# A retention layer and a gated FFN on one core: W3 times W_out moved to the head, 256-token FFN tiles, k padded in place of q

## The chip, the cores and the metric

The kernel runs on one core of a Trainium2 chip. Five engines work side by side, each with an instruction queue of its own that it takes in order: TensorE (PE, matmuls into the eight PSUM banks), VectorE (DVE), ScalarE (ACT), GpSimd (POOL) and SyncE (SP, which issues all loads and stores here). The metric is the device time in microseconds, as the median of several executions.

## The reference

A linear attention over 4 batches, 8 heads, 768 positions and head size 64, with a decay per head, gives `x`; a gated feed-forward follows.

```python
gamma = 1.0 - 2.0 ** (-5.0 - np.arange(H))
for t in range(S):
    state = gamma * state + einsum('bhd,bhe->bhde', k[:, :, t], v[:, :, t])
    y[:, :, t] = einsum('bhd,bhde->bhe', q[:, :, t], state) / sqrt(D)
x = y.transpose(0, 2, 1, 3).reshape(3072, 512)
a, b = x @ w1, x @ w2            # 512 x 1024 each
out = ((a * b) @ w3) @ w_out     # 1024 x 1024, 1024 x 512
```

## The kernel before

The recurrence is cut into 24 steps of 128 positions (6 for each batch). For each, a chunk of q, k and v (256 KB each, in float32) is loaded by `load_chunk(n)`, up to six ahead. `casts(n)` makes float16 copies: q on ScalarE, k on GpSimd, and v times the decay (`vp`, zero-padded per pair of heads) on GpSimd. `transposes(n)` turns q and k with TensorE into one PSUM bank (`psT`); VectorE copies k and q out (`kT`, `qT`), and ScalarE copies q a second time, in two halves of 64 partitions, into a zero-padded `qp`. `scores(n)` multiplies `kT` and `qp` into `psA`, and VectorE masks them (`am`). `kv(n)` makes the new state (`psK`, then `s` on VectorE and `t` on GpSimd); the last step of a batch has none. `outputs(n)` adds both parts in `psY`, the first step of a batch without a state, and VectorE writes them, scaled, into `XT`, which keeps x transposed for all 3072 tokens in float16.

Since nothing stands between w3 and w_out, the kernel multiplies these two first: `w3_transpose(f)` and `w3_mm(f)` make row f of `W3O` (1024 x 512), and the FFN then needs only `out = (a * b) @ W3O`. In units: `a_unit` multiplies a tile of tokens by 128 columns of w1 into one bank (`psF`), which ScalarE copies out (`pa`); `b_unit` does it for w2, and VectorE multiplies `pa` by it straight from the bank (`ht`); `o_unit` multiplies 128 tokens of `ht` by `W3O`, ScalarE scales the result (`osb`), and SyncE stores it. `psF` has three banks, `pa` two buffers.

The order is written out by hand. In the head, chunks 0 and 1 are loaded first, then half of w1 and w2, chunks 2 and 3, the other half, chunks 4 and 5, w_out and w3, through six staging buffers; steps 0 to 5 run among the first three FFN tiles, and then W3O is made in one piece (16 matmul groups in a row). From step 6 on `step(n)` runs a queue of FFN units: it pulls a quarter of its share after the transposes, after the scores, after psK and after psY. Tiles are 256 tokens for the first five and the last, 512 for the three between. `step` places the transposes of n + 1 ahead of the scores of n:

```python
casts(n + 1 + look)
transposes(n + 1)
fill.pull(share * 0.25, ready)
scores(n)
fill.pull(share * 0.25, ready)
t_new = kv(n)
fill.pull(share * 0.25, ready)
outputs(n, t_new)
fill.pull(share * 0.25, ready)
```

Of the kernel before, what the change touches and what calls it, by code (L numbers as in the profile page):

```python
# [18 lines left out]
def kernel(  # L19
# [11 lines left out]
    nc = tc.nc  # L31
    B, H, S, D = q.shape
    C = 128
    NCH = S // C
# [11 lines left out]
    wstage = ctx.enter_context(tc.tile_pool(name="wstage", bufs=6))  # L46
# [34 lines left out]
    def load_w12(half):  # L81

        got = []
        for d in range(4):
            t = new_stage()
            for i, w in enumerate((moe_w1, moe_w2)):
                dma_in(
                    t[:, i * 512 : (i + 1) * 512],
                    w[d * 128 : (d + 1) * 128, half * 512 : (half + 1) * 512],
                )  # L90
            got.append(t)
        return got
# [25 lines left out]

    ident16 = const.tile([128, 128], HP, name="ident16")
# [45 lines left out]
    W12 = [wpool.tile([128, 2, 2, 512], HP, name=f"w12_{i}") for i in range(4)]  # L167
# [11 lines left out]
    def cast_w12(half, got):  # L179
        for d in range(4):  # L180
            cast_to(W12[d][:, half, :, :].rearrange("p a n -> p (a n)"), got[d][:, :], d % 2 == 0)

    def cast_wo(got, i):
        cast_to(WO[i][:, :, :].rearrange("p a n -> p (a n)"), got[i][:, :], False)

    def cast_w3(got, f):
        t = att.tile([128, 1024], HP, tag="w3h", name="w3h", bufs=4)
        cast_to(t[:, :], got[f][:, :], f % 2 == 0)
        W3h[f] = t


    def w3_transpose(f):
        src = W3h.pop(f)
        ps = ps_t.tile([128, 1024], HP, tag="psT", name="psT")
# [4 lines left out]
        t = att.tile([128, 1024], HP, tag="w3t", name="w3t")  # L199
        nc.vector.tensor_copy(t[:, :], ps[:, :])  # L200
        w3t[f] = t

    def w3_mm(f):
# [7 lines left out]
        nc.scalar.copy(W3O[f][:, :], ps[:, :])  # L211


    q16s, k16s, qTs, kTs, ATs = {}, {}, {}, {}, {}
    Tst = [None]

    def casts(n):
# [4 lines left out]
        nc.scalar.copy(q16[:, :], q32[:, :])  # L222
# [13 lines left out]
    def transposes(n):  # L236
# [4 lines left out]
        for p in range(NP):  # L241
            nc.tensor.transpose(ps[:, 0, p, :], q16[:, p * 128 : (p + 1) * 128], ident16[:, :])  # L242
        for p in range(NP):
            nc.tensor.transpose(ps[:, 1, p, :], k16[:, p * 128 : (p + 1) * 128], ident16[:, :])  # L244
        qp = QP[n % 2]
        qT = att.tile([128, NP, 128], HP, tag="qT", name="qT")
        kT = att.tile([128, NP, 128], HP, tag="kT", name="kT")
# [4 lines left out]
        qTs[n], kTs[n] = qT, kT  # L252

    def scores(n):
        kT, qp = kTs.pop(n), QP[n % 2]
        am = att.tile([128, NP, 2, 128], HP, tag="am", name="am")
        for half in range(2):
            ps = ps_at.tile([128, 2, 2, 128], FP, tag=f"psA{half}", name=f"psA{half}")
            for i in range(2):
                p = half * 2 + i  # L260
                nc.tensor.matmul(  # L261
                    ps[:, i, :, :], lhsT=kT[:, p, :], rhs=qp[:, p, :, :], start=True, stop=True
                )
# [44 lines left out]

    class Ffn:
        def __init__(self, tok0, TB, bufs):  # L310
            self.tok0, self.TB, self.bufs = tok0, TB, bufs
            self.HT = None

        def mm(self, which, f):
            half, col = f // 4, (f % 4) * 128
            ps = ps_f.tile([128, self.TB], FP, tag="psF", name="psF")
            for d in range(4):
                nc.tensor.matmul(  # L318
                    ps[:, :], lhsT=W12[d][:, half, which, col : col + 128],
                    rhs=XT[:, d, self.tok0 : self.tok0 + self.TB],  # L320
# [4 lines left out]
        def a_unit(self, f):  # L325
            if self.HT is None:
                TB = self.TB
                self.HT = fsb.tile([128, 8, TB], HP, tag=f"ht{TB}", name=f"ht{TB}", bufs=self.bufs)
            ps = self.mm(0, f)
            self.pa = fsb.tile([128, self.TB], FP, tag="pa", name="pa")  # L330
            nc.scalar.copy(self.pa[:, :], ps[:, :])  # L331

        def b_unit(self, f):
            ps = self.mm(1, f)
            nc.vector.tensor_tensor(self.HT[:, f, :], self.pa[:, :], ps[:, :], MULT)  # L335
# [205 lines left out]
```

## Time and profile before

| what | value |
|---|---|
| time, median of 3 runs | 222.26 us (222.25 to 222.26) |
| the profiled execution's own time | 223.81 us |
| its span, first to last instruction | 222.1 us |
| mean granted TensorE clock | 0.975 of full speed |
| busy: TensorE, VectorE, ScalarE, GpSimd | 194.0, 125.0, 104.0, 65.1 us |
| TensorE in the chain that ended last | 77% of the span |

Busy time adds up what an engine's instructions took; a TensorE at half clock is busy too, and pipelined matmuls overlap in it. The chain follows the work that ended last backwards, at each step to what released it. The granted clock is that of the throttle: 1.00 is 2.4 GHz, 0.50 is 1.2 GHz, a value between is a mean over a stretch that has both.

### The profile page before, as it was taken

How to read it: one execution, taken by the hardware profiler on the slowest of the kernel's cores; microseconds unless marked ns; L12 is line 12 of the kernel's file. 1: busy time of each engine (PE TensorE's matmuls, PEld its weight loads, DVE VectorE, ACT ScalarE, POOL GpSimd, SP SyncE). 2: the span in 40 equal slices, each digit the busy share in tenths (PEclk: the TensorE clock that was granted, in tenths of full speed). 3: DMA queues.
4: the chain of work that ended last, by engine and by line, in shares of the span. 5: the costliest groups of instructions: out<-in, count | busy, mean ns of one | idle time of the engine just before them, and what ended most of it. 6: DMA issues, size and time to landing. Idle time of an engine off the chain costs nothing.

```text
span 222.1 us, 4183 instructions
## 1 busy us (share of the span) xinstructions
PE 194.0 (87%) x1536; PEld 128.3 (58%) x1536; DVE 125.0 (56%) x244; ACT 104.0 (47%) x194; POOL 65.1 (29%) x114
## 2 busy tenths in 40 slices
PE   0366769688999989988999999999999999999992
PEld 0254647577755545677777665665556555457650
DVE  4595655574653334466968877678666654431210
ACT  5333515557733484355465554554654443333231
POOL 5514525120004403324673554542045202000000
PEclk9997976999999999999999999999999999999999
DMA  7999999905999963999459996790630011111212
GB/s 144 241 336 214 283 265 274 400 24 192 282 238 218 222 132 116 260 197 219 65 128 227 204 228 147 182 215 3 146 90 35 17 47 50 47 47 47 97 77 111
DMA packets 82899, 35.91 MB, mean 162 GB/s; under 512 B 75712, under 2 KB 75712, under 8 KB 82880
## 3 DMA queue, kind: packets, MB, share of 16 engines
q1 hardware_dynamic: 82880, 35.66, 68.0%
q8 instruction: 12, 0.20, 0.4%
q14 instruction: 7, 0.06, 0.1%
HBM read 29.36 MB, written 6.29 MB: 161 GB/s over the span
## 4 chain that ended last, share of the span: by engine, by line
PE 77%; ACT 7%; SPq 4%; issue 4%; DVE 4%; DMA 3%; ACTq 0%; DVEq 0%
PE psF L318 35%; PE psO L340 19%; PE psW L207 5%; SPq L60 4%; PE psA L261 4%; DMA q<-in_q_dram 3%; PE psT L242 3%; PE psT L244 2%; ACT qp L251 2%; PE psY L299 2%; PE psY L300 2%; PE psY L302 2%; PE psK L282 2%; PE psT L196 1%; ACT pa L331 1%
## 5 line engine op out<-in xcount | busy, mean ns | idle before, releaser
L318 PE MATMUL psF<-xt,w 128*128 128x256 f16 (+1 forms) x576 | 99.1, 316 | 6.5 <-ACT pa L331 3.0
L318 PEld LDWEIGHTS <-w 128*128 128x128 f16 x576 | 56.1, 101 | 30.7 <-issue 5.7
L335 DVE TENSOR_TENSOR ht<-pa,psF 128x256 f16<-128x256 f32 (+1 forms) x72 | 36.5, 508 | 44.7 <-ACT pa L331 19.9
L331 ACT COPY pa<-psF 128x256 f32<-128x256 f32 (+1 forms) x72 | 31.3, 444 | 33.5 <-PE psF L318 32.4
L340 PE MATMUL psO<-w3o,ht 128*128 128x512 f16 x192 | 45.0, 379 | 0.0
L291 POOL TENSOR_TENSOR t<-s,GS 128x512 f16<-128x512 f32 x16 | 20.3, 1269 | 63.6 <-DVE s L290 48.3
L264 DVE TENSOR_TENSOR am<-psA,keep 128x512 f16<-128x512 f32 x48 | 30.9, 685 | 8.9 <-PE psA L261 8.8
L345 ACT ACTIVATE osb<-psO 128x512 f32<-128x512 f32 x24 | 14.3, 597 | 40.7 <-PE psO L340 39.3
L228 POOL TENSOR_TENSOR vp<-v,VS 128x256 f16<-128x256 f32 x48 | 28.5, 615 | 10.4 <-PE psY L302 4.4
L340 PEld LDWEIGHTS <-ht 128*128 128x128 f16 x192 | 18.3, 98 | 18.6
L224 POOL CAST k<-k 128x512 f16<-128x512 f32 x24 | 14.9, 620 | 45.2 <-DMA k<-in_k_dram 30.7
L250 ACT COPY qp<-psT 64x512 f16<-64x512 f16 x24 | 13.9, 578 | 25.5 <-DVE qT L249 10.7
L261 PE MATMUL psA<-qp,kT 128*128 128x256 f16 x96 | 14.8, 278 | 7.9 <-ACT qp L251 7.1
L248 DVE COPY kT<-psT 128x512 f16<-128x512 f16 x24 | 10.1, 421 | 16.5 <-PE psT L244 16.5
L299 PE MATMUL psY<-am,vp 128*128 128x128 f16 x96 | 17.4, 224 | 1.4 <-DVE am L264 1.0
L303 DVE TENSOR_TENSOR xt<-psY,YS 128x512 f16<-128x512 f32 x24 | 16.5, 687 | 3.0 <-PE psY L302 3.0
L300 PE MATMUL psY<-am,vp 128*128 128x128 f16 x96 | 17.4, 225 | 0.0
L261 PEld LDWEIGHTS <-kT 128*128 128x128 f16 x96 | 9.5, 100 | 12.8 <-issue 7.1
L242 PE MATMUL psT<-ident,q 128*128 128x128 f16 x96 | 10.0, 230 | 7.3 <-ACT q L222 7.3
L207 PE MATMUL psW<-wo,w3t 128*128 128x512 f16 x64 | 15.1, 379 | 0.0
L222 ACT CAST q<-q 128x512 f16<-128x512 f32 x24 | 14.8, 618 | 0.0
L302 PE MATMUL psY<-qT,t 128*128 128x128 f16 x80 | 14.8, 221 | 0.0
(43 smaller groups left out, 157.1 us busy)
## 6 DMA issues: line engine op xcount, KB each, us to landing
q<-in_q_dram SPq DMA_DIRECT2D x24, 256.0 KB, 4.9
k<-in_k_dram SPq DMA_DIRECT2D x24, 256.0 KB, 5.0
v<-in_v_dram SPq DMA_DIRECT2D x24, 256.0 KB, 4.8
out_dram<-osb SPq DMA_DIRECT2D x24, 256.0 KB, 2.0
stg<-in_moe_w_dram SPq DMA_DIRECT2D x16, 256.0 KB, 5.6
stg<-in_moe_w_dram SPq DMA_DIRECT2D x8, 512.0 KB, 5.0
stg<-in_moe_w_out_dram SPq DMA_DIRECT2D x4, 512.0 KB, 6.1
```

Of the source, the lines that this page charges most:

```text
L207: nc.tensor.matmul(ps[:, :], lhsT=t[:, g * 128 : (g + 1) * 128], rhs=WO[g // 2][:, g % 2, :], start=(g == 0), stop=(g == 7),)
L228: nc.gpsimd.tensor_tensor(vp[:, :, r, r * 64 : r * 64 + 64], v32[:, :].rearrange("j (p s e) -> j p s e", s=2, e=64)[:, :, r, :], VS[:, :]. ...
L261: nc.tensor.matmul(ps[:, i, :, :], lhsT=kT[:, p, :], rhs=qp[:, p, :, :], start=True, stop=True)
L264: nc.vector.tensor_tensor(am[:, half * 2 : half * 2 + 2, :, :].rearrange("j p s i -> j (p s) i"), ps[:, :, :, :].rearrange("j p s i -> j ( ...
L291: nc.gpsimd.tensor_tensor(t16[:, :, :], s32[:, :, :], GS[:, :, :], MULT)
L299: nc.tensor.matmul(ps[:, p, :], lhsT=vp[:, p, 0, :], rhs=am[:, p, 0, :], start=True, stop=False)
L300: nc.tensor.matmul(ps[:, p, :], lhsT=vp[:, p, 1, :], rhs=am[:, p, 1, :], start=False, stop=(c == 0))
L302: nc.tensor.matmul(ps[:, p, :], lhsT=Tst[0][:, p, :], rhs=qT[:, p, :], start=False, stop=True)
L318: nc.tensor.matmul(ps[:, :], lhsT=W12[d][:, half, which, col : col + 128], rhs=XT[:, d, self.tok0 : self.tok0 + self.TB], start=(d == 0), ...
L331: nc.scalar.copy(self.pa[:, :], ps[:, :])
L335: nc.vector.tensor_tensor(self.HT[:, f, :], self.pa[:, :], ps[:, :], MULT)
L340: nc.tensor.matmul(psO[:, :], lhsT=self.HT[:, f, tb * 128 : (tb + 1) * 128], rhs=W3O[f][:, :], start=(f == 0), stop=(f == 7),)
```

## The change

The order of the head is new. w3 row 0, w_out, and w3 rows 1 to 4 are loaded first, then chunks 0 and 1, w3 rows 5 to 7, w1 and w2 in whole rows (1024 columns), and chunks 2 to 5; the staging pool has 12 buffers. W3O is made first, with steps 0 and 1 inside it, and its transposes use a `psF` bank. Matmuls on zeros (`busy`, 8 and 10) stand around the first W3 transposes. The first FFN tile runs by rows: all eight column blocks of w1 row d at once, in three `psF` banks and the `psY` bank, then w2 in the same way; ScalarE copies the w1 sums into two staging buffers. From step 2 on all is in the queue, and all tiles have 256 tokens. k is padded (`kp`) by ScalarE's two copies, no longer q, VectorE copies only qT, k is transposed ahead of q, and the scores are 8 matmuls of 128 columns. q is cast on GpSimd.

```diff
-    wstage = ctx.enter_context(tc.tile_pool(name="wstage", bufs=6))
+    wstage = ctx.enter_context(tc.tile_pool(name="wstage", bufs=WST))
...
+    w3_st = [load_rows(moe_w3, 0)]
+    wo_st = [load_wo(i) for i in range(4)]
+    w3_st += [load_rows(moe_w3, f) for f in range(1, 5)]
     load_chunk(0)
     load_chunk(1)
+    w3_st += [load_rows(moe_w3, f) for f in range(5, 8)]
+    w1_st = [load_rows(moe_w1, d) for d in range(4)]
+    w2_st = [load_rows(moe_w2, d) for d in range(4)]
+    for n in range(2, 6):
+        load_chunk(n)
...
-        nc.scalar.copy(q16[:, :], q32[:, :])
+        nc.gpsimd.tensor_copy(q16[:, :], q32[:, :])
...
-        nc.vector.tensor_copy(kT[:, :, :], ps[:, 1, :, :])
+        nc.scalar.copy(kp[0:64, :, 0, :], ps[0:64, 1, :, :])
+        nc.scalar.copy(kp[64:128, :, 1, :], ps[64:128, 1, :, :])
         nc.vector.tensor_copy(qT[:, :, :], ps[:, 0, :, :])
-        nc.scalar.copy(qp[0:64, :, 0, :], ps[0:64, 0, :, :])
-        nc.scalar.copy(qp[64:128, :, 1, :], ps[64:128, 0, :, :])
...
-                nc.tensor.matmul(
-                    ps[:, i, :, :], lhsT=kT[:, p, :], rhs=qp[:, p, :, :], start=True, stop=True
-                )
+                for r in range(2):
+                    nc.tensor.matmul(
+                        ps[:, i, r, :], lhsT=kp[:, p, r, :], rhs=qT[:, p, :], start=True, stop=True
+                    )
...
-    tiles = [(256 * i, 256) for i in range(5)] + [(1280 + 512 * i, 512) for i in range(3)] + [(2816, 256)]
...
+    def busy(m):
+
+        z = VP[0][:, :, :, :].rearrange("p a b c -> p (a b c)")
+        ps = ps_f.tile([128, 512], FP, tag="psF", name="psZ")
+        for _ in range(m):
+            nc.tensor.matmul(ps[:, :], lhsT=z[:, 0:128], rhs=z[:, 0:512], start=True, stop=True)
...
+    busy(8)
+    w3_transpose(0)
+    busy(10)
+    w3_mm(0)
+    w3_transpose(1)
...
+    w3_transpose(5)
+    cast_w3(6)
+    transposes(1)
+    outputs(0, t_new)
+    w3_transpose(6)
+    cast_w3(7)
+    scores(1)
+    w3_mm(5)
+    t_new = kv(1)
+    w3_transpose(7)
     outputs(1, t_new)
...
+    w3_mm(6)
...
+    w3_mm(7)
...
+    def by_rows(W, ps, d):
+        for f in range(8):
+            nc.tensor.matmul(
+                ps[f // 2][:, f % 2, :], lhsT=W[d][:, f * 128 : (f + 1) * 128],
+                rhs=XT[:, d, 0:TB], start=(d == 0 and f % 2 == 0),
+                stop=(d == 3 and f % 2 == 1),
+            )
+
+    ps = four_banks()
+    for d in range(4):
+        by_rows(W1, ps, d)
...
+    for i in range(4):
+        nc.scalar.copy(pa[i], ps[i])
     casts(2)
+    ps = four_banks()
+    for d in range(4):
+        by_rows(W2, ps, d)
+        if d == 1:
+            transposes(2)
+            casts(3)
+    for i in range(4):
+        nc.vector.tensor_tensor(f0.HT[:, 2 * i : 2 * i + 2, :], pa[i], ps[i], MULT)
...
+    for t in range(1, NT):
+        late = ffn[t - 1].o_units() if t > 1 else []
+        for f in range(8):
+            fill.units += ffn[t].ab_units(f)
+            if f % 4 == 3 and late:
                 fill.units.append(late.pop(0))
```

On SyncE, the head of the program before: the loads of chunks 0 and 1 and of the first half of w1 and w2 (`stg` is a staging buffer, `x8` eight of a kind).

```order
L60 DMA q_87<-in_q_dram 128x8x64
L60 DMA k_89<-in_k_dram 128x8x64
L60 DMA v_91<-in_v_dram 128x8x64
L60 DMA q_93<-in_q_dram 128x8x64
L60 DMA k_95<-in_k_dram 128x8x64
L60 DMA v_97<-in_v_dram 128x8x64
L60 DMA stg<-in_moe_w_dram 128x512 x8
```

The same place of the changed program, up to the load of chunk 2's q:

```order
L61 DMA stg<-in_moe_w_dram 128x1024
L61 DMA stg<-in_moe_w_out_dram 128x2x512 x4
L61 DMA stg<-in_moe_w_dram 128x1024 x4
L61 DMA q_105<-in_q_dram 128x8x64
L61 DMA k_107<-in_k_dram 128x8x64
L61 DMA v_109<-in_v_dram 128x8x64
L61 DMA q_111<-in_q_dram 128x8x64
L61 DMA k_113<-in_k_dram 128x8x64
L61 DMA v_115<-in_v_dram 128x8x64
L61 DMA stg<-in_moe_w_dram 128x1024 x11
L61 DMA q_139<-in_q_dram 128x8x64
```

Nine weight loads went ahead of chunk 0, and eleven (w3 rows 5 to 7, w1, w2) between chunk 1 and chunk 2.

On ScalarE, one step of before with 256-token tiles in its queue, from the cast of q to that of the next step:

```order
L222 CAST q_1304<-q_1114 128x512
L250 COPY qp_100<-psT 64x4x128
L251 COPY qp_100<-psT 64x4x128
L331 COPY pa<-psF 128x256 x4
L222 CAST q_1416<-q_1203 128x512
```

One step of the changed program, from one `osb` to the next:

```order
L334 ACTIVATE osb<-psO 128x512
L237 COPY kp_163<-psT 64x4x128
L238 COPY kp_163<-psT 64x4x128
L318 COPY pa<-psF 128x256 x4
L334 ACTIVATE osb<-psO 128x512
```

The q cast has left ScalarE, and the padded copies stand right behind the eviction of an `o` unit.

On VectorE, the same step of before:

```order
L248 COPY kT<-psT 128x512
L249 COPY qT<-psT 128x512
L335 TENSOR_TENSOR ht_1325<-pa,psF 128x256
L264 TENSOR_TENSOR am<-psA_1340,keep 128x512
L264 TENSOR_TENSOR am<-psA_1344,keep 128x512
L335 TENSOR_TENSOR ht_1325<-pa,psF 128x256
L290 TENSOR_TENSOR s_1367<-psK,t_1268 128x512
L335 TENSOR_TENSOR ht_1325<-pa,psF 128x256
L303 TENSOR_TENSOR xt<-psY,YS 128x4x128
L335 TENSOR_TENSOR ht_1325<-pa,psF 128x256
```

And of the changed program:

```order
L239 COPY qT<-psT 128x512
L324 TENSOR_TENSOR ht<-pa,psF 128x256
L253 TENSOR_TENSOR am<-psA_1454,keep 128x512
L253 TENSOR_TENSOR am<-psA_1460,keep 128x512
L324 TENSOR_TENSOR ht<-pa,psF 128x256 x2
L279 TENSOR_TENSOR s_1491<-psK,t_1365 128x512
L324 TENSOR_TENSOR ht<-pa,psF 128x256
L292 TENSOR_TENSOR xt<-psY,YS 128x4x128
```

The copy of k is gone, and the products move: two of them follow the masks directly, and none stands behind `xt`. On TensorE such a step is now: transposes of k, of q, units a, b, a, scores, units b, a, b, psK, units a, b, psY, one `o` unit; this repeats in steps 6 to 22. Steps 2 and 3 have transposes, scores, one `o` unit, psK and psY.

## Rows read from the trace of the kernel before

**Rows 1.** The page: busy time of each engine, and the chain by engine.

```profile
PE 194.0 (87%) x1536; PEld 128.3 (58%) x1536; DVE 125.0 (56%) x244; ACT 104.0 (47%) x194; POOL 65.1 (29%) x114
...
PE 77%; ACT 7%; SPq 4%; issue 4%; DVE 4%; DMA 3%; ACTq 0%; DVEq 0%
```

**Rows 2.** Table of stretches; columns as in its first line.

```profile
core 0: us, PE busy (x) PEld busy (x) DVE busy (x) ACT busy (x) POOL busy (x), PEclk, DMA share, GB/s
...
20.00:25.00 5.00, 4.49 (x36) 3.65 (x37) 2.19 (x6) 2.44 (x6) 2.99 (x5) 0.67 1.09 228
25.00:30.00 5.00, 3.15 (x41) 2.70 (x39) 3.91 (x9) 1.53 (x3) 1.27 (x1) 1.00 1.04 337
30.00:35.00 5.00, 4.11 (x24) 2.87 (x22) 1.85 (x4) 0.84 (x3) 2.59 (x4) 0.51 1.19 219
```

**Rows 3.** Timeline of the head: start, duration, engine, line, idle before.

```profile
4.55 0.60 ACT L222 CAST q<-q 128x512 f16<-128x512 f32 x1
...
14.01 1.04 ACT L177 CAST w<-stg 128x1024 f16<-128x1024 f32 x1 [0.21 <-DMA stg<-in_moe_w_dram]
...
18.10 0.39 PE L318 MATMUL psF<-xt,w 128*128 128x256 f16 x2 [2.00 <-DVE w L175]
```

**Rows 4.** Chain that ended last, in order of time: start, duration, what.

```profile
66.04 0.45 PE psT L196 x8
...
200.73 1.75 PE psF L318 x16
...
212.89 5.20 PE psO L340 x24
...
218.16 0.60 ACT osb L345
```

**Rows 5.** Timeline of one attention step with 256-token tiles.

```profile
94.03 0.39 PE L244 MATMUL psT<-ident,k 128*128 128x128 f16 x4
94.05 0.60 ACT L345 ACTIVATE osb<-psO 128x512 f32<-128x512 f32 x1 [2.02 <-PE psO L340]
...
94.45 0.42 DVE L248 COPY kT<-psT 128x512 f16<-128x512 f16 x1 [1.48 <-PE psT L244]
94.55 0.61 ACT L222 CAST q<-q 128x512 f16<-128x512 f32 x1
...
94.79 0.41 DVE L249 COPY qT<-psT 128x512 f16<-128x512 f16 x1
...
95.30 0.58 ACT L250 COPY qp<-psT 64x512 f16<-64x512 f16 x1
95.56 0.60 PE L318 MATMUL psF<-xt,w 128*128 128x256 f16 x4
...
96.49 0.65 ACT L331 COPY pa<-psF 128x256 f32<-128x256 f32 x2
96.89 0.42 DVE L335 TENSOR_TENSOR ht<-pa,psF 128x256 f16<-128x256 f32 x1 [1.69 <-ACT pa L331]
96.91 0.60 PE L318 MATMUL psF<-xt,w 128*128 128x256 f16 x4 [0.75 <-ACT pa L331]
...
97.23 1.28 DVE L264 TENSOR_TENSOR am<-psA,keep 128x512 f16<-128x512 f32 x2
...
97.57 1.04 PE L318 MATMUL psF<-xt,w 128*128 128x256 f16 x8
98.21 0.37 ACT L331 COPY pa<-psF 128x256 f32<-128x256 f32 x1 [1.07 <-PE psF L318]
...
98.43 0.41 DVE L335 TENSOR_TENSOR ht<-pa,psF 128x256 f16<-128x256 f32 x1
```

**Rows 6.** Table of stretches of one microsecond, chunk loads and weight loads.

```profile
6.00:7.00 1.00, 0.61 (x4) 0.34 (x4) 0.67 (x6) 0.00 (x0) 0.34 (x1) 1.00 1.39 217
...
41.00:42.00 1.00, 0.03 (x1) 0.00 (x0) 0.00 (x0) 0.95 (x2) 0.00 (x0) 1.00 1.08 404
```

**Rows 7.** Groups of instructions by line and shape: count, busy us, mean ns, idle before.

```profile
L224 POOL CAST k<-k 128x512 f16<-128x512 f32 x24 | 14.9, 620 | 45.2 <-DMA k<-in_k_dram 30.7 <-PE psK L282 11.0 <-issue 3.5
...
L175 DVE CAST w3h<-stg 128x1024 f16<-128x1024 f32 x4 | 2.7, 685 | 0.0
```

More of the change, by code (lines that the diff above doesn't have):

```diff
@@ L210, in w3_mm @@
             )
[L211 to L214 removed]
+        cast_to(W3O[f][:, :], ps[:, :], f < 2)
+    q16s, k16s, qTs, ATs = {}, {}, {}, {}
     Tst = [None]
@@ L386, in run, with step @@
                 self.units.pop(0)[2]()
+    NT = NTOK // TB
     fill = Queue()
-    def step(n, look=1):
+    def step(n):
         ready = n * C
-        nxt = next((t0 + tb for t0, tb in tiles if t0 + tb > ready), NTOK)
-        share = fill.available(ready) / max(1, nxt // C - n)
-        casts(n + 1 + look)
+        share = fill.available(ready) / (2 - n % 2)
+        casts(n + 2)
         transposes(n + 1)
@@ L421 @@
     outputs(0, t_new)
+    w3_transpose(6)
+    cast_w3(7)
     scores(1)
+    w3_mm(5)
     t_new = kv(1)
+    w3_transpose(7)
     outputs(1, t_new)
-    cast_w12(0, w12a)
-    wo_st = load_wo()
-    w3_st = [load_w3(f) for f in range(8)]
-    f0 = Ffn(*tiles[0], 4)
-    fill.units = f0.ab_units(range(0, 4))
-    fill.run(2)
-    casts(2)
-    transposes(2)
-    fill.run(2)
-    scores(2)
-    casts(3)
-    fill.run(1)
-    t_new = kv(2)
-    fill.run(1)
-    transposes(3)
-    outputs(2, t_new)
@@ L442 @@
-    fill.run(2)
-    scores(3)
-    t_new = kv(3)
-    outputs(3, t_new)
-    f1 = Ffn(*tiles[1], 4)
-    fill.units = f1.ab_units(range(0, 4))
-    fill.run(4)
-    cast_w12(1, w12b)
-    fill.run(4)
-    fill.units = f0.ab_units(range(4, 8)) + f1.ab_units(range(4, 8))
-    fill.run(2)
-    casts(4)
-    transposes(4)
-    fill.run(2)
-    scores(4)
-    fill.run(2)
-    casts(5)
-    t_new = kv(4)
-    fill.run(2)
-    transposes(5)
-    outputs(4, t_new)
-    fill.run(2)
-    scores(5)
-    fill.run(2)
@@ L495 @@
-    fill.units = f0.o_units() + f1.o_units() + f2.o_units()
-    late = []
-    for i, (tok0, TB) in list(enumerate(tiles))[3:]:
-        f = Ffn(tok0, TB, 4 if TB == 256 else 2)
-        for j in range(0, 8, 2):
-            fill.units += f.ab_units((j, j + 1))
-            if late:
+    cast_w(W1, w1_st, 0, False)
+    cast_w(W1, w1_st, 1, True)
+    w3_mm(6)
+    cast_w(W1, w1_st, 2, False)
+    cast_w(W1, w1_st, 3, True)
+    w3_mm(7)
+    for d in range(4):
+        cast_w(W2, w2_st, d, True)
@@ new lines, with four_banks @@
+    ffn = [Ffn(t) for t in range(NT)]
+    f0 = ffn[0]
+    hold = [new_stage() for _ in range(2)]
+    f0.HT = fsb.tile([128, 8, TB], HP, tag="ht", name="ht", bufs=3)
+    def four_banks():
+        got = [ps_f.tile([128, 2, TB], FP, tag="psF", name="psF") for _ in range(3)]
+        last = ps_at.tile([128, NP, 128], FP, tag="psY", name="psYf")
+        return [t[:, :, :] for t in got] + [last[:, :, :].rearrange("p (a b) c -> p a (b c)", a=2)]
+    def by_rows(W, ps, d):
[4 more added lines that the diff above has]
+                stop=(d == 3 and f % 2 == 1),
+            )
@@ L502 @@
+    fill.units = f0.o_units()
+    for t in range(1, NT):
[3 more added lines that the diff above has]
+            if f % 4 == 3 and late:
                 fill.units.append(late.pop(0))
-        fill.units += late
-        late = f.o_units()
-    fill.units += late
-    for n in range(6, NSTEP):
+    fill.units += ffn[NT - 1].o_units()
+    for n in range(2, NSTEP):
         load_chunk(n + 4)
```

170 lines of the change are left out of this document (66 added, 104 removed).

## Prediction

> **What bounds the kernel now.** Read first the busy time and the chain that ended last [rows 1]. TensorE is 77% of the chain and busy for 194.0 of 222.1 us, so the question is where TensorE stands still or runs at the lower clock. The table of stretches answers where: at 20 to 25 us it had a granted clock of 0.67, at 30 to 35 us one of 0.51, half speed, though it counted as busy [rows 2]. The timeline of the head shows why it started late: the first chunk is cast at 4.55, the first weight tile at 14.01, and the first matmul of the FFN starts at 18.10 [rows 3]. The later part reads differently: from 200.73 on the chain is matmuls end to end, 16 of 256 columns in 1.75 us, 24 of 512 columns in 5.20 us, then 0.60 us of the last eviction [rows 4]. In between lies the attention step with 256-token FFN tiles, where TensorE waits 0.75 us for a `pa` copy of ScalarE [rows 5]. So there are three stretches with a limit of their own: the head (loads, casts, clock), the steps (ScalarE's and VectorE's queues), the end (TensorE alone).
>
> **Prices.** From the chain [rows 4]: eight 128-column transposes 0.45 us, so 0.056 each; a unit (4 matmuls of 256 columns) 0.44; an `o` unit or one `w3_mm` (8 of 512) 1.73. From the step [rows 5], start to start on one engine: `osb` to the next ScalarE copy 0.50 (94.05, 94.55); two padded copies 1.19 (95.30 to 96.49); one `pa` copy 0.37, the next 0.28 after its start (two in 0.65); VectorE's copy of 128x512 0.34 (94.45, 94.79); a product over 256 columns 0.42, the next instruction 0.34 later (96.89, 97.23); two masks 1.20 (97.23 to 98.43), so 0.60 for anything over 512 columns in f32. From one engine to the next: a unit is read 0.64 after its start (97.57, 98.21), transposes 0.42 after the start of the last four (94.03, 94.45), and TensorE takes a bank 0.05 after the copy out of it ended (96.86, 96.91).
>
> **The change, part by part: the head.** Loads are ordered anew, and their rates come from stretches with one kind of load: q, k, v move at 217 GB/s, weights at 404 [rows 6], so 1.20 us for one 256 KB tensor and 1.30 for 512 KB of weights. The first tensor is cast at 4.55, which leaves 3.35 us for issue and latency. In the new order w3 row 0 is there at 4.65, all of w_out at 9.9, w3 rows 1 to 4 by 15.1, chunks 0 and 1 by 22.3, w3 rows 5 to 7 by 26.2, w1 by 31.4, w2 by 36.6, chunks 2, 3, 4, 5 at 40.2, 43.8, 47.4, 51.0. Up to row 5's landing at 23.55 TensorE has 12.0 us of work (five rows of 1.73 + 0.45, chunk 0's transposes, scores and psK) after w_out's last cast at about 10.6 (VectorE's cast takes 0.685 [rows 7]); it is ready for row 5, with some 2 us to spare. The 18 matmuls on zeros fill idle time; they cost nothing unless they outlast w_out's casts.
>
> From there a chain, each link a price above: row 5 cast on ScalarE (1.04 [rows 3]) 24.65; its transposes, chunk 1's, chunk 0's psY 26.0; row 6's cast is behind one eviction on ScalarE, so its transposes end at 26.75; chunk 1's padded k and qT follow that cast, scores end at 28.4; row 5's product 30.1; psK, row 7's transposes, psY 31.45; two products 34.95. The first tile waits until the last product's bank is evicted (35.8), and its four w1 rows of 8 x 0.109 end at 38.9. Then all four banks must be copied out by ScalarE, 0.50 apart, before w2's first row can end at 40.8; three more rows and chunk 2's transposes, 43.9; four VectorE products of 512 columns, 46.3. Steps 2 and 3 have only tile 0's two `o` units to fill them: step 2 ends at 48.35, since its masks wait behind those products, step 3 at 52.2, and `xt` of chunk 3, which tile 1 needs, at 53.1. So step 4 counts as begun at 52.65. The loads alone would let it begin no earlier than 51.0: chunk 5's k at 49.8 and two GpSimd casts of 0.62 [rows 7]. Above it, the clock: one fall as at 20 to 25 us cost 0.33 x 5 = 1.7 us [rows 2], and the new head has gaps too (w_out's arrival, the four evictions, the HT products). I take 1.0 for it: 53.65. Bounds: 51.0 with no further loss, 58 with three such falls on the path.
>
> **The steps.** The 20 steps from 4 on hold 8 units each (256-token tiles throughout), from step 6 one `o` unit too. TensorE's work in a full step: transposes 0.45, 8 units 3.50, scores 0.45, psK 0.22, psY 0.67, `o` 1.73 = 7.01 us. Scores become 8 matmuls of 128 columns instead of 4 of 256: 8 x 0.056 = 0.45 against 0.44, no change. Two 256-column matmuls for one of 512 cost 1.75 against 1.73 for 16 and 8 [rows 4], in all 0.45 us on 192 matmuls; it is in the unit's price. The Trainium skill (Perfetto Trace Analysis, Matmuls) says that larger matmuls are more efficient where they are possible, which speaks against the 256-token tiles. The trace agrees in sign, and its price on TensorE is those 0.45 us; what smaller tiles do to the copies is worked out next.
>
> What TensorE waits for is worked out as a schedule of one step, from the first k transpose at 0, after an `o` unit that ended there. ScalarE: `osb` 0.24 (94.05; that step began 0.22 before 94.03), padded copies of k 0.75 and 1.34 to 1.93 (no wait for VectorE and no q cast ahead, unlike before), `pa` 1 1.93 to 2.30, `pa` 2 to 2.58. VectorE may copy qT only after ScalarE's two copies: 1.98; product 1 2.33 to 2.75; masks 2.66 and 3.26; product 2 3.86 to 4.28. TensorE: a, b, a until 1.76, scores 2.20; the fourth unit needs the bank of the first, free at 2.35 (0.15 lost); third pair and psK until 3.89; then the next unit needs the bank of product 2, 4.33 (0.44 lost). So a step lasts 7.60, 0.59 of it lost: three banks cannot cover masks that stand ahead of a product. Before, the same rules put `pa` 1 at 2.69 after the step's start, where it is [rows 5].
>
> The q cast on GpSimd costs nothing: 0.620 there for k, 0.61 on ScalarE [rows 5, 7], and GpSimd's busy time goes from 65.1 to some 80 us of the span [rows 1]; if that cover were gone, transposes would come 0.62 late. Sum: step 4 5.28, step 5 (no psK) 5.06; steps 6 to 22, 17 x 7.01 less 5 x 0.22 (three without state, two without psK) = 118.05, and 17 x 0.59 = 10.0 lost; step 23 6.7; the last tile and four `o` units 7.0 + 6.9 = 13.9. Together 159.0.
>
> **Sum.** 53.65 + 159.0, and behind TensorE's end 4.0 as before (222.1 - 218.1 [rows 4]): a span of 216.7 against 222.1. The profiled execution lasted 223.81, 1.7 us beyond its span and 1.55 above the median of 222.26, so span and median differ by 0.16: 216.8 us. The head gives most of it, the steps take some back.
>
> **Rivals.**
> *No loss in the steps.* If ScalarE's earlier start frees the banks in time, the 10 us shrink to under 2: 208.5 us. For it: ScalarE loses a cast and a wait of 0.8 per step. Against it: the 0.44 is lost on VectorE's order, which the change leaves.
> *As much loss as before.* In the step of [rows 5] TensorE stood from 96.00 to 96.91, 0.91 us. If that stays in all 17 full steps, 17 x 0.32 more: 222.2 us, no change. For it: the same three banks. Against: the copies begin earlier here.
> *The clock stays low in the head (slower).* Between 10 and 45 us TensorE has some 24 us of work at full clock. A microsecond at half clock costs 0.5, and the first 2 us of loss may fall where there is time to spare. The forecast holds 1.0; slower than before starts at about 14 us at the lower clock (215.8 + 7 = 222.8), 18 if the spare time takes its part. Before, the two stretches alone had 8 us of it (0.33 and 0.49 of 5 us [rows 2]); 20 us would give 224 to 226 us. The Trainium skill (TensorE: Matmul & The Clock Gate, Part 1) has the low clock as the state from which sustained matmuls lift TensorE; the trace agrees so far as the clock of 0.51 stands behind a stretch in which TensorE was busy for 3.15 of 5 us [rows 2]. For this rival are the gaps behind the zeros; against it, that from row 5's landing on the gaps are about a microsecond each.
> *The new order changes nothing in the head.* If loads bind rather than TensorE, step 4 begins at 51.0 in any case: 214.1 us.
>
> **How the numbers follow.** Likeliest, 0.60: loss per step of 0.3 to 0.85 and step 4 at 51 to 57, 212 to 221 us, with 216.8 in it; the load-bound head is inside this. No loss in the steps 0.15; as much loss as before 0.12; low clock 0.13. The range is 209.0 to 222.6: it leaves out half of the first rival and most of the last. About 0.2% (0.45 us) is what a measurement of this kernel can tell from no change. Faster takes the likeliest, the first rival and half of the second, 0.81; no change 0.06; slower 0.13.
>
> **What would show it.** The first full step's transposes near 64 us (53.65 + 10.3); steps of 7.6 us with a wait on a VectorE product just after psK; W3's last product near 35 us; w2's first row held up by four ScalarE copies; the granted clock at 1.00 from about 45 us. The prediction is wrong if full steps are close to 7.0 or above 7.9, or if step 4 begins beyond 58.

## The result, and the profile after

The changed kernel takes 211.39 us (median of 4 runs, 210.48 to 211.56) against 222.25 us for the one before: a ratio of 0.951, 95% interval 0.948 to 0.954. The forecast was 216.8 us: faster, as it is, and 5.4 us too high. The profiled execution lasted 211.31 us with a span of 209.6 us and a mean granted clock of 0.992.

The page gives the busy time of each engine and the chain that ended last by engine, to be held against [rows 1]:

```profile
PE 196.6 (94%) x1842; PEld 147.7 (70%) x1842; DVE 116.7 (56%) x242; ACT 91.3 (44%) x188; POOL 78.6 (37%) x138
...
PE 84%; DVE 4%; DMA 4%; ACT 4%; issue 1%; SPq 1%; DVEq 0%; ACTq 0%
```

TensorE has 2.6 us more of busy time than before and 12.5 us less of span. VectorE and ScalarE are relieved by 8.3 and 12.7 us, GpSimd has 13.5 us more, close to the 80 us of the forecast.

The table of stretches (columns as in its first line) answers to [rows 2], now for the head of the new order:

```profile
core 0: us, PE busy (x) PEld busy (x) DVE busy (x) ACT busy (x) POOL busy (x), PEclk, DMA share, GB/s
10.00:15.00 5.00, 2.56 (x7) 0.96 (x8) 1.29 (x2) 2.95 (x4) 0.00 (x0) 0.75 1.04 404
15.00:20.00 5.00, 4.56 (x38) 2.66 (x37) 2.59 (x5) 2.01 (x2) 1.35 (x3) 0.91 1.12 221
20.00:25.00 5.00, 5.00 (x37) 2.76 (x36) 1.27 (x2) 1.92 (x4) 3.42 (x6) 1.00 1.10 296
```

The lower clock comes once, at 10 to 20 us, and not again; from 20 us on every stretch has 1.00. The timeline of TensorE's head (start, duration, line, idle time before) shows what was running there:

```profile
6.11 2.32 PE L398 MATMUL psZ<-vp 128*128 128x512 f16 x10
12.44 3.54 PE L197 MATMUL psW<-wo,w3t 128*128 128x512 f16 x8 [4.00 <-DVE w3t L190]
...
17.36 1.90 PE L197 MATMUL psW<-wo,w3t 128*128 128x512 f16 x8 [0.44 <-DVE w3t L190]
```

After the zeros TensorE stands for 4.00 us, and the first product of W3O then takes 3.54 us where the second takes 1.90. The first steps of the chain in order of time (start, duration, what) say why it starts at 12.44, and the later ones give the pace of the steps:

```profile
2.73 8.34 DMA stg<-in_moe_w_out_dram
...
11.09 0.69 DVE wo L169
...
33.28 3.47 PE psW L197 x16
...
40.54 1.58 ACT stg L470 x3
...
54.71 1.03 PE psF L308 x8
...
64.84 0.22 PE psT L232 x4
...
71.69 0.22 PE psT L232 x4
...
78.80 0.22 PE psT L232 x4
...
85.92 0.22 PE psT L232 x4
...
200.28 5.19 PE psO L329 x24
```

w_out's last load lands at 11.07 (2.73 + 8.34), W3's last product ends at 36.75, the first FFN unit of step 4 starts at 54.71. From 71.69 on the transposes of k come every 7.11 us: that is a full step, of which the forecast made 7.60. One such step, in the timeline (as [rows 5]):

```profile
78.84 0.60 ACT L334 ACTIVATE osb<-psO 128x512 f32<-128x512 f32 x1 [2.48 <-PE psO L329]
...
79.33 0.57 ACT L237 COPY kp<-psT 64x512 f16<-64x512 f16 x1
...
79.91 0.58 ACT L238 COPY kp<-psT 64x512 f16<-64x512 f16 x1
...
80.52 0.65 ACT L318 COPY pa<-psF 128x256 f32<-128x256 f32 x2
80.53 0.42 DVE L239 COPY qT<-psT 128x512 f16<-128x512 f16 x1 [2.72 <-ACT kp L238]
...
80.94 1.47 PE L308 MATMUL psF<-xt,w 128*128 128x256 f16 x12
...
81.26 1.28 DVE L253 TENSOR_TENSOR am<-psA,keep 128x512 f16<-128x512 f32 x2
...
82.25 0.39 PE L271 MATMUL psK<-vp,k 128*128 128x128 f16 x4
...
82.46 0.74 DVE L324 TENSOR_TENSOR ht<-pa,psF 128x256 f16<-128x256 f32 x2
82.47 1.05 PE L308 MATMUL psF<-xt,w 128*128 128x256 f16 x8
```

The row to look at is the last. The unit behind psK was to wait 0.44 us until VectorE's second product had emptied its bank; it starts at 82.47, 0.22 after psK's start and right behind it, 0.01 us after that product has only begun (82.46). ScalarE and VectorE are where the schedule of the prediction has them: taking 78.64, the start of the first k transpose, as 0, the `osb` starts at 0.20 (forecast 0.24), the first `pa` copy at 1.88 (1.93), qT at 1.89 (1.98), the second product at 3.82 (3.86). Only the bank is another one. The 0.09 us by which the first unit behind the scores starts late (80.94, against 80.40 + 0.45) is all that such a step loses.

Which bank a unit gets can be read from what its first matmul waits for. TensorE's rows in program order around psK, in the changed kernel (`w_0_225` is of w1, `w_0_229` of w2; of each unit only the first weight load and matmul are shown, and "waits" names the engine whose semaphore is waited for):

```
1052 L271 MATMUL psK<-vp_165,k_827 128x128
1053 L308 LDWEIGHTS w_0_225
1054 L308 MATMUL psF<-xt,w_0_225 128x256 [waits Activation_49]
...
1061 L308 LDWEIGHTS w_0_229
1062 L308 MATMUL psF<-xt,w_0_229 128x256 [waits DVE_49]
```

The a-unit (1054) waits for ScalarE and the b-unit (1062) for VectorE: the a-unit gets the bank of the previous a-unit, which a `pa` copy empties, and not the bank next in turn, which stands behind the masks and a product. The unit behind psK waits for ScalarE in all 15 of the steps 6 to 22 that have a psK. The prediction took the three banks in turn.

### The profile page after: what moved, and what is told of

It is laid out like the page before. It is cut to its first block, busy times and chain, and to the rows that moved or that the text cites. A ratio compares the mean times of both kernels' runs of the same rounds, so it can differ in the third digit from the quotient of the medians.

```text
span 209.6 us, 4835 instructions
## 1 busy us (share of the span) xinstructions
PE 196.6 (94%) x1842; PEld 147.7 (70%) x1842; DVE 116.7 (56%) x242; ACT 91.3 (44%) x188; POOL 78.6 (37%) x138
## 4 chain that ended last, share of the span: by engine, by line
PE 84%; DVE 4%; DMA 4%; ACT 4%; issue 1%; SPq 1%; DVEq 0%; ACTq 0%
PE psF L308 38%; PE psO L329 18%; PE psW L197 7%; PE psA L250 5%; DMA stg<-in_moe_w_out_dram 4%; PE psT L232 2%; PE psT L234 2%; PE psY L288 2%; PE psY L289 2%; PE psY L291 2%; PE psF L459 2%; PE psK L271 2%; ACT stg L470 1%; DVE am L253 1%; ACT kp L238 1%
## 5 line engine op out<-in xcount | busy, mean ns | idle before, releaser
L308 PE MATMUL psF<-xt,w 128*128 128x256 f16 x704 | 87.5, 272 | 0.4 <-DVE xt L292 0.3
L308 PEld LDWEIGHTS <-w 128*128 128x128 f16 x704 | 67.0, 97 | 9.8 <-issue 1.0
L318 ACT COPY pa<-psF 128x256 f32<-128x256 f32 x88 | 31.1, 373 | 36.5 <-PE psF L308 36.0
L239 DVE COPY qT<-psT 128x512 f16<-128x512 f16 x24 | 10.2, 425 | 56.7 <-ACT kp L238 56.7
L324 DVE TENSOR_TENSOR ht<-pa,psF 128x256 f16<-128x256 f32 x88 | 35.1, 416 | 10.8 <-ACT pa L318 6.1
L212 POOL CAST q<-q 128x512 f16<-128x512 f32 x24 | 14.6, 610 | 22.1 <-DMA q<-in_q_dram 19.2
L197 PE MATMUL psW<-wo,w3t 128*128 128x512 f16 x64 | 16.6, 410 | 4.4 <-DVE w3t L190 4.4
L237 ACT COPY kp<-psT 64x512 f16<-64x512 f16 x24 | 13.7, 571 | 6.5 <-PE psT L234 6.5
L250 PE MATMUL psA<-qT,kp 128*128 128x128 f16 x192 | 14.6, 219 | 1.0 <-DVE qT L239 0.9
L197 PEld LDWEIGHTS <-w3t 128*128 128x128 f16 x64 | 6.2, 103 | 11.9 <-DVE w3t L190 5.1
L238 ACT COPY kp<-psT 64x512 f16<-64x512 f16 x24 | 13.9, 580 | 0.4
```

Of the source, the lines that this page charges most:

```text
L197: nc.tensor.matmul(ps[:, :], lhsT=t[:, g * 128 : (g + 1) * 128], rhs=WO[g // 2][:, g % 2, :], start=(g == 0), stop=(g == 7),)
L250: nc.tensor.matmul(ps[:, i, r, :], lhsT=kp[:, p, r, :], rhs=qT[:, p, :], start=True, stop=True)
L308: nc.tensor.matmul(ps[:, :], lhsT=W[d][:, f * 128 : (f + 1) * 128], rhs=XT[:, d, self.tok0 : self.tok0 + TB], start=(d == 0), stop=(d == 3),)
L318: nc.scalar.copy(self.pa[f][:, :], ps[:, :])
L324: nc.vector.tensor_tensor(self.HT[:, f, :], self.pa.pop(f)[:, :], ps[:, :], MULT)
```

## The experiments

Two theories stood at the start. Mine: the steps decide, a step's length is set by when ScalarE and VectorE hand back the `psF` banks, and the forecast was high because of one wrong bank. Rival: the whole gain comes from the head, and the steps only run at TensorE's pace because units wait for nothing any more. The kernel before took 222.25 to 222.32 us (medians) beside all of these runs. The diffs are against the changed kernel unless the text says otherwise; "..." marks what is left out.

### The steps

**Banks strictly in turn.** The `psF` pool is split into three single banks that are handed out one after the other (every request for a `psF` tile now goes through `bank`); nothing else changes.

```diff
-    ps_f = ctx.enter_context(tc.tile_pool(name="ps_f", bufs=3, space=PSUM))
+    ps_f = ctx.enter_context(tc.tile_pool(name="ps_f", bufs=1, space=PSUM))
+    turn = [0]
+
+    def bank(shape, dt, name):
+        turn[0] += 1
+        return ps_f.tile(shape, dt, tag=f"psF{turn[0] % 3}", name=name)
...
```

> The changed kernel with its three psF banks handed out strictly in turn. Theory: the loss of 0.44 us that the prediction put into each full step came from this assumption alone, and it did not happen because the pool gave the fourth a-unit a bank that ScalarE had emptied. In turn, that unit waits behind psK for VectorE's second product: a full step of 7.5 to 7.6 us instead of 7.11, 17 steps, 218 to 220 us. Rival: ScalarE's earlier copies leave enough time whatever the bank; then the time stays within 0.5 us of 211.4.

It took 219.05 us (218.46 to 219.33), ratio 0.984 (0.979 to 0.989), and its steps last 7.55 us (first k transposes at 79.97 and 87.52). Its timeline has the wait that the prediction described, at the place where it put it:

```profile
83.59 0.39 PE L276 MATMUL psK<-vp,k 128*128 128x128 f16 x4
...
83.79 0.74 DVE L329 TENSOR_TENSOR ht<-pa,psF 128x256 f16<-128x256 f32 x2
84.25 1.03 PE L313 MATMUL psF<-xt,w 128*128 128x256 f16 x8 [0.27 <-DVE ht L329]
```

The unit starts 0.66 us after psK's start instead of 0.22. In program order its first matmul now waits for VectorE, in each of the 15 steps. 17 steps of 0.44 us make 7.5 of the 7.66 us. So the one bank is worth what the forecast charged for it, and the changed kernel doesn't pay it.

**q padded again.** q is transposed first, VectorE copies kT and qT, ScalarE pads q, and the scores are 4 matmuls of 256 columns again (eleven staging buffers, so that kT has room).

```diff
...
-        nc.scalar.copy(kp[0:64, :, 0, :], ps[0:64, 1, :, :])
-        nc.scalar.copy(kp[64:128, :, 1, :], ps[64:128, 1, :, :])
...
+        nc.vector.tensor_copy(kT[:, :, :], ps[:, 1, :, :])
         nc.vector.tensor_copy(qT[:, :, :], ps[:, 0, :, :])
...
+        nc.scalar.copy(qp[0:64, :, 0, :], ps[0:64, 0, :, :])
+        nc.scalar.copy(qp[64:128, :, 1, :], ps[64:128, 0, :, :])
...
```

> The changed kernel with q padded again (VectorE copies kT and qT, then ScalarE copies q twice; scores are 4 matmuls of 256 columns; one staging buffer less for room). Theory: ScalarE's copies start 0.75 us later in a step, the first pa copy with them, and the fourth unit waits for its bank: about 7.85 us per full step, 222 to 226 us. Rival: which of the two is padded does not matter, since three banks and the o unit cover it: 211 to 213 us.

It took 226.59 us (226.41 to 227.61), ratio 1.020 (1.013 to 1.026): slower than the kernel before. A step lasts 7.92 us (first k transposes at 73.58 and 81.50).

```profile
82.27 0.41 DVE L239 COPY qT<-psT 128x512 f16<-128x512 f16 x1
...
82.77 0.58 ACT L240 COPY kp<-psT 64x512 f16<-64x512 f16 x1 [0.69 <-PE psF L309]
...
83.97 0.65 ACT L319 COPY pa<-psF 128x256 f32<-128x256 f32 x2
...
84.39 1.47 PE L309 MATMUL psF<-xt,w 128*128 128x256 f16 x12 [0.75 <-ACT pa L319]
```

ScalarE's first padded copy starts 0.09 us after VectorE's second copy has ended (82.68), having stood for 0.69. The profile names a unit on TensorE (L309) as the releaser, but that row of the program waits for VectorE, whose two copies read the same bank and stand ahead in the program; in the changed kernel it is VectorE that waits for ScalarE. Behind it the `pa` copies are late, and TensorE waits 0.75 us for a bank, exactly the wait of [rows 5].

**q cast on ScalarE again.** One line, everything else as changed.

```diff
-        nc.gpsimd.tensor_copy(q16[:, :], q32[:, :])
+        nc.scalar.copy(q16[:, :], q32[:, :])
```

> The changed kernel with the q cast back on ScalarE. Theory: it stands between osb and the padded copies, so the pa copy comes 0.5 us later and TensorE waits for it: about 7.6 us per full step, 218 to 221 us. Rival: ScalarE has half of each step free, so the cast is hidden: 211 to 212 us.

It took 219.60 us (219.12 to 221.48), ratio 0.9885 (0.986 to 0.991), with steps of 7.63 us (73.05 and 80.68); a unit waits 0.46 us for the `pa` copy:

```profile
81.38 0.61 ACT L212 CAST q<-q 128x512 f16<-128x512 f32 x1
...
83.08 0.65 ACT L318 COPY pa<-psF 128x256 f32<-128x256 f32 x2
...
83.51 1.47 PE L308 MATMUL psF<-xt,w 128*128 128x256 f16 x12 [0.46 <-ACT pa L318]
```

So a cast of 0.61 us off ScalarE is worth 8.2 us here, since in each of the steps it stands ahead of the `pa` copies.

**Both undone: the attention part of before.** The two edits above together.

> The changed kernel with the whole attention part of before: q padded again and q cast on ScalarE again (eleven staging buffers in place of twelve). Theory: with q padded, ScalarE's padded copies must wait for VectorE's two copies out of the same bank (in the trace of before they start 0.10 us after VectorE's second copy ends), and the cast stands in that wait; so it costs next to nothing on top of the 226.59 us that q padded alone took: 227 to 229 us. Rival: the two costs add up, 226.59 + (219.60 - 211.39) = 234.8 us.

It took 227.28 us (226.41 to 227.75), ratio 1.020 (1.016 to 1.024). The costs don't add up to the rival's 234.8: with q padded, the cast is worth 0.7 us, less than the spread of either kernel's runs. The trace shows where it goes:

```profile
91.70 0.61 ACT L212 CAST q<-q 128x512 f16<-128x512 f32 x1
...
91.99 0.41 DVE L239 COPY qT<-psT 128x512 f16<-128x512 f16 x1
...
92.50 0.58 ACT L240 COPY kp<-psT 64x512 f16<-64x512 f16 x1 [0.19 <-PE psF L309]
...
94.12 1.47 PE L309 MATMUL psF<-xt,w 128*128 128x256 f16 x12 [0.75 <-ACT pa L319]
```

ScalarE would have had to wait for VectorE's copy until 92.40 anyway; the cast fills that wait and leaves 0.19 of it. The step is again 7.92 us long (91.23 and 99.15).

### How much is the steps', how much the head's

**The attention part alone, in the kernel before** (k padded, k transposed first, 8 score matmuls, q cast on GpSimd; head and tiles of before), the diff against that kernel:

```diff
-        nc.scalar.copy(q16[:, :], q32[:, :])
+        nc.gpsimd.tensor_copy(q16[:, :], q32[:, :])
...
-        nc.vector.tensor_copy(kT[:, :, :], ps[:, 1, :, :])
+        nc.scalar.copy(kp[0:64, :, 0, :], ps[0:64, 1, :, :])
+        nc.scalar.copy(kp[64:128, :, 1, :], ps[64:128, 1, :, :])
         nc.vector.tensor_copy(qT[:, :, :], ps[:, 0, :, :])
-        nc.scalar.copy(qp[0:64, :, 0, :], ps[0:64, 0, :, :])
-        nc.scalar.copy(qp[64:128, :, 1, :], ps[64:128, 0, :, :])
...
```

> The kernel before with only the attention part of the change: k padded in place of q, k transposed first, scores in 8 matmuls, q cast on GpSimd. Theory: the waits for a pa copy in the steps with 256-token tiles (0.75 and 0.53 us each, some five steps) shrink, and in the head scores no longer wait for the second padded copy as long: 217.5 to 219.5 us; most of the change's 10.9 us is the new head. Rival: the steps of before were covered by their o units and 512-token tiles, and the head waits for loads anyway: 221.5 to 222.5 us.

217.11 us (216.58 to 218.11), ratio 0.975 (0.970 to 0.980). A little better than the expectation of my theory.

**Tiles of before in the changed kernel** (five of 256, three of 512, one of 256; ten staging buffers):

```diff
-    NT = NTOK // TB
+    tiles = [(256 * i, 256) for i in range(5)] + [(1280 + 512 * i, 512) for i in range(3)] + [(2816, 256)]
+    NT = len(tiles)
...
```

> The changed kernel with the tile sizes of before (five of 256 tokens, three of 512, one of 256; two HT buffers and ten staging buffers for room). Theory: a full step loses only 0.1 us either way, and 96 units of 512 columns fewer instructions are worth 0.35 us: 210.5 to 212.5 us, no difference that counts. Rival, from the rule that larger matmuls are more efficient: 209.5 us or less; or the other way, that 512-column copies hold three banks longer: 213 us or more.

210.31 us (209.9 to 210.9), ratio 0.944 (0.940 to 0.948): some 1.1 us below the changed kernel. The 256-token tiles gain nothing under the new attention part; the prediction charged them 0.45 us. Some 0.7 of the 1.1 us lies behind the head: from the first k transpose of step 6 to the span's end this trace takes 144.2 us (63.98 to 208.2), that of the changed kernel 144.9 (64.67 to 209.6; starts by the timeline, a little ahead of the chain's 64.84).

**The head alone**: the attention part and the tiles of before in the changed kernel, that is the three diffs (q padded, q cast, tiles) together.

> The same with the tiles of before (five of 256 tokens, three of 512, one of 256; ten staging buffers): what is left of the change is the order of the head alone. Theory: the head is worth what it is worth under the new attention part, 217.11 - 210.31 = 6.8 us, so 222.3 - 6.8 = 215.5 us (214.5 to 217.0). Rival: the new head leaves more FFN units to the steps, where the old attention part makes each wait, so that the gain of the head is lost again: 219 to 223 us.

216.17 us (215.78 to 216.63), ratio 0.970 (0.966 to 0.974), 0.7 us from the expected 215.5. The rival falls. The six kernels make a table (us):

| | head of before | new head, tiles of before | new head, 256-token tiles |
|---|---|---|---|
| attention part of before | 222.25 | 216.17 | 227.28 |
| new attention part | 217.11 | 210.31 | 211.39 |

With the tiles of before the two parts add up: the attention part gives 5.1 and 5.9 us, the head 6.1 and 6.8. The tiles don't: 256 tokens throughout cost 1.1 us under the new attention part and 11.1 under the old one. The number of staging buffers, which differs (twelve in the changed kernel, ten or eleven in the other three with the new head), is not what does it: they serve the head alone, and w2's last row lands at 37.66 with ten of them (new attention part, tiles of before) and at 38.52 with twelve. The groups of TensorE's instructions at 130 to 175 us show why (columns as in [rows 7]); first the old attention part with 256-token tiles, then with those of before:

```profile
L309 PE MATMUL psF<-xt,w 128*128 128x256 f16 x189 | 23.7, 272 | 4.6 <-ACT pa L319 4.5
```

```profile
L307 PE MATMUL psF<-xt,w 128*128 128x512 f16 x112 | 27.4, 379 | 0.0
```

With 256 columns in a unit TensorE waits 4.5 us for `pa` copies in these 45 us; with 512 it waits for nothing, though the attention part is the same. From step 6 on, the loss of the old attention part lies in the steps with 256-token tiles alone, and the change spreads those over the whole kernel. With the tiles of before, steps 6 to 9, which have 256-token tiles, take 31.5 us under the old part (67.80 to 99.28) and 28.2 under the new one (63.98 to 92.18), steps 10 to 21 70.9 and 70.7. The other 3.8 us were there at step 6; 1.4 of them is a first W3O product that started later in that execution (13.14 against 11.72).

### The head

**No zeros**: both calls of `busy` are left out.

```diff
-    busy(8)
     w3_transpose(0)
-    busy(10)
```

> The changed kernel without its 18 matmuls on zeros. Theory: they end at about 8.4 us, TensorE then stands still until w_out is cast at 12.4, and the first product ran at half clock in spite of them; without them the head is at most 1.5 us later: 211.4 to 213 us. Rival: they lift the clock for the W3 products, and without them these run at half clock for longer: 214 us or more.

211.15 us (210.89 to 212.05), ratio 0.950 (0.944 to 0.954): no difference from 211.39. Without zeros W3O's first product took 3.60 us (at 12.91), with them 3.54: in these two traces the ten do nothing for it. It is not so in every execution. In four other traces with the same zeros (q padded, q cast on ScalarE, both, and the tiles of before) TensorE stood for 2.56 to 3.28 us ahead of that product and it took 1.90 (in the remaining four 2.49 to 3.55); with the tiles of before:

```profile
11.72 1.90 PE L197 MATMUL psW<-wo,w3t 128*128 128x512 f16 x8 [2.56 <-DVE w3t L190]
```

That the zeros bought this clock isn't shown, since the kernel without them has one trace alone; in the time they make no difference.

**More zeros**: 28 in place of 10, so that they last until w_out is there.

```diff
-    busy(10)
+    busy(28)
```

> The changed kernel with 28 matmuls on zeros behind the first W3 transposes instead of 10, so that they last until w_out is cast. Theory: the first W3 product, 3.5 us at half clock, takes 1.7 us, and TensorE's chain up to chunk 1's padded copies is 1 to 1.7 us earlier; what reaches the end is 0.5 to 1.5 us: 210 to 211 us. Rival: the chain behind it waits for loads and casts that are not earlier, or the zeros outlast w_out's casts: 211.2 us or more.

210.94 us (210.32 to 211.56), ratio 0.947 (0.943 to 0.951). The granted clock stays at 1.00 and the first product takes 1.89 us:

```profile
6.09 6.21 PE L398 MATMUL psZ<-vp 128*128 128x512 f16 x28
12.14 1.89 PE L197 MATMUL psW<-wo,w3t 128*128 128x512 f16 x8
```

That product ends about 2 us earlier than in the changed kernel, yet W3's last two products start only 0.59 earlier (32.69 against 33.28) and step 4's first unit 0.59 (54.12 against 54.71). Its chain shows what was next in line, the load of w3 row 5 and that row's cast on ScalarE:

```profile
18.41 6.33 DMA stg<-in_moe_w_dram
...
24.82 1.04 ACT w3h L171
```

In the changed kernel that load landed at 24.80 and the cast started at 25.33, so 0.5 us is all that an earlier TensorE could gain there. The difference in time, 0.45 us, is less than the spread of either kernel's runs.

**The first tile in ordinary units** in place of whole rows in four banks:

```diff
...
+    for f in range(8):
+        fill.units += f0.ab_units(f)
     casts(2)
+    fill.run(8)
+    transposes(2)
+    casts(3)
+    fill.run(8)
...
```

> The changed kernel with the first tile in 16 ordinary units (a, b in turn in the psF banks) in place of w1 and w2 by rows in four banks. Theory: w1 and w2 are cast by the time TensorE comes to them, so rows gain no earlier start, while w2's first row waits about 1 us for four copies and the o units wait for four products at the end; units spread both: 1 to 2.5 us faster, 209 to 210.5 us. Rival: rows follow the casts as they come, and units, which need all four rows at once, start later: 212 us or more.

211.62 us (210.74 to 212.55), ratio 0.949 (0.945 to 0.954): no difference. The gain that my theory saw in doing without the four ScalarE copies isn't there: the first unit starts at 36.56, but the second needs all of w2, whose last load lands at 38.32, so TensorE goes on only at 39.09, and step 4's first unit comes at 54.94. Rows and units are worth the same.

**Two of those four copies on VectorE**, which does nothing from 39.2 to 45.1 us:

```diff
     for i in range(4):
-        nc.scalar.copy(pa[i], ps[i])
+        (nc.vector.tensor_copy if i % 2 else nc.scalar.copy)(pa[i], ps[i])
```

> The changed kernel with the second and fourth of the four copies of the w1 sums on VectorE instead of ScalarE. Theory (TensorE's order in the head sets when step 4 begins): VectorE does nothing between 39.2 and 45.1 us in the trace of the changed kernel, so two engines empty the four banks in about half the time; w2's first row, 40.70 to 42.5 there, ends about 0.8 us earlier, everything behind it moves with it, step 4's first unit comes at 53.9 instead of 54.71, and the time is 210.6 us instead of 211.39. Rival (the loads of chunks 3 to 5 or ScalarE's padded copies set it): the first unit of step 4 stays at 54.6 to 54.8 and the time at 211.2 to 211.6.

211.09 us (210.33 to 211.62), ratio 0.949 (0.945 to 0.953): inconclusive. In its trace w2's first row passes the copies faster, but the row started 0.38 us later in this execution (41.08 against 40.70), and step 4's first unit comes at 54.55, 0.16 us earlier. An effect of about half a microsecond can't be told in the time.

**Tiles of before, more zeros and the two copies together**, the three diffs in one kernel:

> Three edits together: the tiles of the kernel before (five of 256, three of 512, one of 256 tokens), 28 instead of 10 matmuls on zeros, and the two copies on VectorE. Theory: each acts at a place of its own. The tiles gave 1.1 us alone (210.31 against 211.39), the zeros 0.45 (210.94), the copies 0.8 by the expectation of the run that has them alone; the sum is 2.3 us, a time of 209.1 us (208.6 to 209.6). Rival: the first two both take their microsecond from the same slack in the head (step 4's first unit was at 54.02 and 54.12 in these two runs, at 54.71 without them), so that they don't add up: 209.7 to 210.4 us.

210.40 us (209.28 to 210.94), ratio 0.945 (0.941 to 0.950): the rival was right, the three don't add up. The chain before step 4 in the trace, of the slowest of these executions (210.94):

```profile
45.12 5.45 DMA v<-in_v_dram
...
50.64 1.16 POOL vp L218 x2
51.79 1.08 POOL t L280
...
54.29 0.69 DVE xt L292
...
55.02 1.03 PE psF L306 x8
```

With TensorE earlier, the head ends with a load: v of chunk 4 lands at 50.57, GpSimd makes its `vp` ahead of the `t` of step 2, which step 3 needs, and `xt` follows. It is a bound by loads, as the prediction had one at 51.0 us, but by another load: the forecast had all of chunk 4 in place by 47.4. No version here beats the changed kernel by more than the 1.1 us of the tiles of before. In this trace too the stretch from step 6 on takes 144.2 us (64.99 to 209.2), against 144.9 to 145.1 in the kernels with the changed kernel's steps; so some 0.7 us of it is the tiles', and the rest a head that comes out differently from execution to execution (step 4's first unit at 54.02 with the tiles of before alone, at 55.02 here).

## Why the forecast was right in sign and 5.4 us high

**The step that failed** is the loss in the steps: "then the next unit needs the bank of product 2, 4.33 (0.44 lost)". It was read as if `psF`'s three banks went round in turn; the program gives that unit a bank which ScalarE empties. Measured against its terms:

| term | forecast | measured | difference |
|---|---|---|---|
| first transposes of step 6 | 63.95 | 64.84 | +0.9 |
| steps 6 to 22, to the end of step 22's `o` unit | 128.05 | 120.21 (64.84 to 185.05) | -7.8 |
| step 23, last tile, `o` units, to TensorE's end | 20.6 | 20.4 (to 205.47) | -0.2 |
| behind TensorE | 4.0 | 4.1 | +0.1 |
| span | 216.7 | 209.6 | -7.1 |

The work of a step was right (7.01; the chain's pieces give 7.11 with 0.09 lost on the fourth unit, where 0.15 was forecast). The bank run turns the failed step on by itself: steps of 7.55 and 219.05 us. By its own test, full steps close to 7.0, the prediction was wrong here, and 211.39 lies below its likeliest 212 to 221 us; the range took the time in because it kept half of a rival. So it was the rival "no loss in the steps" (208.5 us, chance 0.15) that came true for the steps; what spoke against it, "the 0.44 is lost on VectorE's order, which the change leaves", was a wait read from a wrong bank.

**The head** was 0.9 us late by step 6, and its pieces are off by more. w_out landed at 11.07 instead of 9.9, and the first product took 1.8 us longer at the lower clock, 3.0 together. The spare time ahead of row 5 took up most of that. Row 5 was cast at 25.33 instead of 23.6; of these 1.7 us, 1.2 is the row's own load, which landed at 24.80 instead of 23.55, and at 24.74 with more zeros, where TensorE was earlier; only the last 0.5 is ScalarE, still at chunk 0's padded copies behind the late transposes. W3's last product ended at 36.75 instead of 34.95, w2's first row at 42.54 (40.8), the first tile's HT products at 47.93 (46.3). Of this lateness of 1.6 to 1.8 us the forecast had 1.0 as its allowance for the clock. But by the run with more zeros the clock's part is 0.59, and the loads' is the larger: w1's last row landed at 33.3 (31.4), w2's at 38.5 (36.6), chunk 4 at 49.0 (47.4). One load behind another they kept the forecast's pace (1.28 us for a row, 1.30 forecast), but with gaps that the sum doesn't have, as between w_out's first two loads, which landed at 5.49 and 8.36 by the profile's account; why the gaps are there isn't shown.

The first product took 3.54 us after 4.00 us of standing and 1.89 where zeros bridged the gap. The Trainium skill (TensorE: Matmul & The Clock Gate, Part 1) has the low clock as the state from which sustained matmuls lift TensorE; these two rows agree with it. Removing this loss gave at most half a microsecond, since the load and the cast of row 5 were next in line.

**Other points.** The four ScalarE copies do hold w2's first row up (1.58 us in the chain), and removing them changes nothing that can be measured. The q cast costs nothing on GpSimd, as said; what the prediction doesn't say is that leaving ScalarE is worth 8.2 us if k is padded too. "The head gives most of it, the steps take some back" was wrong: with the tiles of before, head and attention part give about the same, and the tiles take 1.1 back. With 256-token tiles the new head and the old attention part took 227.28 us, more than the kernel before, so there the attention part is what makes the change faster. The sign wasn't luck, but the size was closer than its parts: the kernel that the forecast described, with banks in turn, took 219.05 us, 2.3 more than forecast, and head and conversion (below) hid that much of the 7.7 us that the bank was wrong by.

**The conversion.** The sum was made against an execution of before that lay 1.55 us above its median, and that distance was carried over as if it belonged to the change. The profiled execution after lies at its median (211.31 and 211.39), so 1.6 of the 7.1 us didn't show in the time. Of the executions of before beside these runs, those with a span of 221.9 to 222.2 us had a mean granted clock of 0.974 to 0.976, as the profiled one, those with 220.6 one of 0.996 or more. A mean of 0.996 leaves less than 2 us at the lower level (0.004 x 220.6 x 2), so the prediction's 8 us at the lower clock are not in all of them. The clock alone doesn't order them, though: the shortest, 219.7 to 220.0 us, had 0.988 to 0.990, and no trace shows why.

## What to carry to other kernels

Before a wait for a bank is put into a sum, read in program order which engine the first matmul of that unit waits for; this pool of three banks did not hand them out in turn, and the difference was 0.44 us in each of 17 steps. What an instruction costs on an engine depends on what stands next to it: the same cast was worth 0.7 us, within the spread of the runs, where it filled a wait and 8.2 where it pushed the copies behind it, so edits that touch the same queue are to be tried alone and together. Where several chains end within a microsecond of each other, as in this head, shortening one gives the next one the lead.

## What was not expected of the hardware

GpSimd casts 128x512 from float32 to float16 as fast as ScalarE: 0.610 us a piece over 24 on the page of the changed kernel, 0.61 on ScalarE with the cast put back. And ten matmuls on zeros that ended 4 us ahead of the first product left it as slow as none did (3.54 and 3.60 us), where in four other traces the same ten, with a gap of 2.56 to 3.28 us, were followed by a product of 1.90; 28 that lasted up to it brought 1.89.
